# The float32 first chunk of a fused attention, Fourier-mixing and FFN kernel made one token tile instead of two, the leftover tile put last, and the sums of the weights' squares given a PSUM bank of their own

## The chip, the cores and the metric

The kernel runs on one NeuronCore of a Trainium2 chip, as one launch. The metric is the device time of the launch in microseconds (us). The engines of the core work side by side, each through a queue of its own in a fixed order: PE (TensorE: matmuls, with the weight loads PEld beside them), DVE (VectorE), ACT (ScalarE), POOL (GpSimd) and SP (SyncE, which only issues transfers here). An instruction starts when those ahead of it on its engine are through and the semaphores that it waits for have come.

## The reference, cut to what matters

```
a    = softmax(phi over the sequence)                 # B=8, H=8, S=576, M=32
k_m  = a^T k ;  v_m = a^T v                           # 32 memories a head
attn = softmax(q k_m^T / sqrt(64)) v_m                # -> x: (8, 576, 512)
u    = x + real(FFT over the sequence, then over the 512 features)
un   = (u - mean(u)) / sqrt(var(u) + 1e-6)            # over the features
out  = u + relu(un @ w_ch1) @ w_ch2                   # 512 -> 2048 -> 512
```

All inputs are float32 and so is the output. 8 x 576 tokens make 36 tiles of 128 tokens.

## The kernel before, in words

**Number formats.** Most products are made of float16 pairs: each operand is a high part and a low part, and three matmuls (high-high, high-low, low-high) stand for one. Both weights must for that be split into pairs, after a scaling by a power of two that is found from the sum of their squares. This takes time at the start, so the first chunk of the FFN, chunk 0, is computed in float32 straight from the unsplit weights.

**The weights.** `w_ch1` and `w_ch2` come in 8 slices each (j = 0 to 7, 128x1024 elements), as 64-bit words that are taken apart. `prepare_w1(j)` and `stage_w2(j)` call `to_f32`: ACT (L931, L935) and DVE (L937, L941, L942, L951) put a float32 slice together, ACT squares it (L957), a matmul with a matrix of ones adds the squares over the partitions (`all_sum`, L240), and `norm_scale` (L258, L266, L269 on DVE) makes the scale. `split_w1(j)` writes the float16 pair of a `w_ch1` slice (high on ACT L973, low on DVE L974), `prepare_w2` that of a `w_ch2` slice (high on ACT L1004, low on DVE L1009, or on POOL for the slices in `L2`). The scale of `w_ch2` (`scale_w2`, L993 to L997) needs all 16 sums. Three staging areas are reused from slice to slice, so that a load waits for the DVE to be through with an earlier slice.

**The FFN.** The 36 tiles are taken in chunks of `CH = 2`, 18 chunks. For each j, `ffn1` makes 256 hidden features (tile `ph`, pool `ps1` with two buffers), an eviction writes them as a float16 pair to `hring` (ACT L870, then DVE L871), and `ffn2` adds their part to the output (`po`, pool `ps2` with two buffers, one for each tile). In chunk 0 `ffn1_direct` and `ffn2_direct` do this in float32, with one ACT eviction (L830). `finish` adds `u` (DVE L892) and sends the tile out.

**The background.** `background` is a generator that makes the tiles `u`, batch by batch: pooling weights (`pf`, `pt_e`), memories (`pm`), scores (`psc`), value transforms (`pv`), spectra (`pa`, copied to `at` by ACT L686 and DVE L688; `vh` likewise from `pv` by L651 and L652), and the mixing (`pp`, `px`, added by DVE L755 and L769). `advance` moves it on between FFN steps. `norm_chunk` normalises a chunk's tiles (`norm_tile`) and transposes them. Batches 0 and 1 keep float32 in the memories and scores. The PSUM pool `psg` (4 buffers, tag `g`) is the ring of all of these; the sums of squares, `as_sq`, take a buffer of it each.

**Order.** A scheduler (with a model of its own of the engines) fixes the order of each engine's queue; `issue_after` and the lists `GATE1`, `GATE2`, `SUMS` and `EARLY` put instructions behind named marks, such as `un1`, the normalisation of tile 1. `keep_busy` issues matmuls whose result nobody uses, to fill TensorE early in the program.

Of the kernel before, what the change touches and what calls it, by code (L numbers as in the profile page):

```python
# [46 lines left out]
GATE1[2] = ["un1", "uh0"]  # L47
SUMS = {8: ["as1_6", "as2_6"], 9: ["as1_7", "as2_7"]}
GATE2 = [[], ["un1", "qs0"]] + [["un1", f"ev{j - 2}"] for j in range(2, 8)]
# [88 lines left out]
def kernel(  # L138
# [659 lines left out]
    def norm_chunk(c):  # L798

        unT = unring[:, c % 2]  # L800
        unT0 = unT.rearrange("p l t k c -> p (l t k c)").bitcast(F32)
        unT0 = unT0.rearrange("p (k t c) -> p k t c", k=NK, t=CH)
        for i in range(CH):
            idx = CH * c + i
            norm_tile(idx, us[idx], un[:, i])
            if c == 0:
                pt = psg.tile([P, 512], F32, tag="g", name=f"pt_unT_{i}")
                for k in range(NK):
                    nc.tensor.transpose(pt[:, k * P : (k + 1) * P], un[:, i, k * P : (k + 1) * P], identf)
                marks["uh0"] = nc.scalar.copy(out=unT0[:, :, i], in_=pt.rearrange("p (k c) -> p k c", k=NK))  # L810
        if c == 0:
            return unT0
        marks[f"uh{c}"] = nc.scalar.copy(out=ud[:, 0], in_=un)  # L813
        marks[f"ul{c}"] = (nc.vector if c == 1 else nc.gpsimd).tensor_tensor(out=ud[:, 1], in0=un, in1=ud[:, 0], op=ALU.subtract)  # L814
        transpose(
            unT.rearrange("p l t k c -> p (l t k) c"), ud.rearrange("p l t c -> p (l t c)"), False, f"unT_{c}"
        )
        return unT

    def ffn1_direct(j):  # L820

        w = w1_f32(j).rearrange("p (k c) -> p k c", k=NK)
        h = h_f32(j)
        for f in range(UB):
            ph = ps1.tile([P, CH, P], F32, tag="h", name=f"ph_0_{j}_{f}", padded_shape=[P, 4, P])
            for k in range(NK):
                marks[f"f1_{j}"] = nc.tensor.matmul(  # L827
                    ph, lhsT=w[:, k, f * P : (f + 1) * P], rhs=unTs[0][:, k], start=(k == 0), stop=(k == NK - 1)
                )
            marks[f"ev{j}"] = nc.scalar.activation(h[:, f], ph, AF.Relu)  # L830
# [4 lines left out]
    def h_f32(j):  # L835
        h = hring[:, 4 + j % 2].rearrange("p l f c -> p (l f c)").bitcast(F32)
        return h.rearrange("p (f t c) -> p f t c", f=UB, t=CH)

    def ffn2_direct(j, po):
        w = w2_f32(j).rearrange("p (a c) -> p a c", a=UB)  # L840
        h = h_f32(j)
        for f in range(UB):
            for t in range(CH):
                marks[f"f2_{j}"] = nc.tensor.matmul(  # L844
                    po[t],
                    lhsT=h[:, f, t],
                    rhs=w[:, f],
                    start=(j == 0 and f == 0),
                    stop=(j == NW - 1 and f == UB - 1),
                )  # L850

    def ffn1(c, unT, j, hs):

        ph = ps1.tile([P, UB, CH, P], F32, tag="h", name=f"ph_{c}_{j}")
        mm = groups()
        for f in range(UB):
            i = 0
            for k in range(NK):
                for lw, lu in ((0, 0), (0, 1), (1, 0)):
                    mm(  # L860
                        ph[:, f],
                        lhsT=w1t[:, j, lw, k, f * P : (f + 1) * P],
                        rhs=unT[:, lu, :, k],
                        start=(i == 0),
                        stop=(i == 3 * NK - 1),
                    )
                    i += 1
        h = h_slot(c, j)
        phv = ph.rearrange("p f t c -> p (f t) c")
        marks[f"ev{c}_{j}"] = nc.scalar.activation(h[:, 0], phv, AF.Relu)  # L870
        nc.vector.scalar_tensor_tensor(  # L871
            out=h[:, 1], in0=phv, scalar=0.0, in1=h[:, 0], op0=ALU.max, op1=ALU.subtract
        )
        hs.append(h)

    def ffn2(c, j, hs, po):
        for f in range(UB):
            for t in range(CH):
                for i, (lh, lw) in enumerate(((0, 0), (0, 1), (1, 0))):
                    nc.tensor.matmul(  # L880
                        po[t],
                        lhsT=hs[j][:, lh, f * 2 + t],
                        rhs=w2s[:, j * UB + f, lw, :],
                        start=(j == 0 and f == 0 and i == 0),
                        stop=(j == NW - 1 and f == UB - 1 and i == 2),
                    )

    def finish(c, po):
        for t in range(CH):
            idx = CH * c + t  # L890
            u = us.pop(idx)
            nc.vector.scalar_tensor_tensor(out=u, in0=po[t], scalar=cout if c else 0.5, in1=u, op0=ALU.mult, op1=ALU.add)  # L892
            nc.sync.dma_start(out=out[idx], in_=u)
# [30 lines left out]
    def to_f32(stages, dst, key):  # L924
# [51 lines left out]
    def prepare_w1(j):  # L976
# [4 lines left out]
        with tc.issue_after(marks["un1"].ins):  # L981
# [5 lines left out]
    def stage_w2(j):  # L987
        top = to_f32(parts_w2.pop(j), w2_f32(j), f"2_{j}")
        with tc.issue_after(marks["un1"].ins):
# [23 lines left out]

    marks = {}
    held = [False]
    ahls = {}
    us = {}
    n_tiles = B * S // P
    n_chunks = n_tiles // CH
# [3 lines left out]
    def background():  # L1023
# [3 lines left out]
        for b in range(B):  # L1027
# [24 lines left out]
            for step in range(NG + 2) if b > 0 else ():  # L1052
# [25 lines left out]
            for t in (0, 1, 2) if b % 2 == 0 else (2, 0, 1):  # L1078
                yield nt, 2 if t < 2 else 1 - b % 2
                if t == 2:  # L1080
                    if b % 2 == 0:
# [3 lines left out]
                        nt += 1  # L1085
# [4 lines left out]
                    add_mix(u2, rows, px, igx, tm, 0)  # L1090
                    continue
                pp = ahead or mix_pp(b, f"t{t}", slice(t * P, (t + 1) * P), full, at, vh)
                ahead = None
                tm = mix_m(full, *pp, isg, isg)
                for sign in range(2):
                    c0 = (2 * t + sign) * P
                    px = mix_x(b, f"t{t}{sign}", c0, P, full, attnT, vbd)
# [5 lines left out]
                if b == 0 and t == 0:  # L1103
                    with tc.issue_after(marks["px"].ins):
                        ahead = mix_pp(b, "t1", slice(P, 2 * P), full, at, vh)
                    keep_busy(28, 2 * P, "norm", behind=marks["pp"])
# [36 lines left out]
    gate = ["un1", "uh0"]  # L1143
# [8 lines left out]
    while made < 2:  # L1152
# [5 lines left out]
    po = [ps2.tile([P, 512], F32, tag="o", name=f"po_0_{t}") for t in range(CH)]  # L1158
    for j in range(NW):
# [9 lines left out]
        if made >= 2 * CH and 1 not in unTs:  # L1169
# [19 lines left out]
    advance(CH, CH * 3)  # L1189
    unTs[2] = norm_chunk(2)  # L1190
    for n in range(NW, n_steps):
        c, j = divmod(n, NW)
        if j == 0:
            po = [ps2.tile([P, 512], F32, tag="o", name=f"po_{c}_{t}") for t in range(CH)]
        ffn2(c, j, hs[c], po)
        run_ffn1(n + 4 if n + 4 <= 2 * NW else n + NHS)
        if j < NW - 1:
            advance(CH * c, steps=1)
        else:
            finish(c, po)  # L1200
            if c + 2 < n_chunks:
                advance(CH * (c + 1), CH * (c + 3))
# [65 lines left out]
```

## Time and profile before

| what | value |
| --- | --- |
| device time, median of 3 runs | 946.54 us (946.08 to 947.56) |
| the profiled execution's own time | 946.59 us |
| its span, first to last instruction | 944.7 us |
| mean granted TensorE clock | 0.996 |
| busy: PE / PEld / DVE / ACT / POOL | 931.0 / 660.5 / 575.8 / 465.2 / 222.7 us |
| first float32 matmul of chunk 0 (`ph` L827) | 55.47 us after the span's start |
| first float16 matmul of chunk 1 (`ph` L294) | 130.6 us |
| first low part of a `w_ch2` slice (DVE L1009) | 144.75 us |
| last matmul ends | 940.2 us |

The profiled execution is within 0.05 us of the median, and 1.9 us of its time lie around its span. Times of instructions are counted from the span's start. A line number stands for a line of the kernel before, unless the text says that it is of the changed kernel. L294 is the line of a helper that issues matmuls in groups, so the tile's name tells what is computed there. "PE busy" counts a matmul from start to a modelled end; matmuls overlap, so the time that one takes in a full queue is that of a stretch divided by its count.

### The profile page before, as it was taken

The numbers are of one execution on the slowest core, as the hardware profiler recorded it, in microseconds if no ns is written. First come the engines' busy times: TensorE is split into PE (matmuls) and PEld (weight loads), VectorE is DVE, ScalarE is ACT, GpSimd is POOL, SyncE is SP. The second block draws the span as 40 slices with busy tenths as digits, with TensorE's granted clock in tenths as the row PEclk, the third lists the DMA queues.
The fourth block names the chain that finished last, engine by engine and source line by source line (L and its number), as shares of the span: only waits on it lengthen the run. The fifth ranks groups of instructions, "written<-read, shape, count | busy, mean of one in ns | idle before, by whom it ended". The sixth has DMA issues, their size and how long they took to land.

```text
span 944.7 us, 18855 instructions
## 1 busy us (share of the span) xinstructions
PE 931.0 (99%) x7742; PEld 660.5 (70%) x7742; DVE 575.8 (61%) x1309; ACT 465.2 (49%) x917; POOL 222.7 (24%) x251
## 2 busy tenths in 40 slices
PE   7899999999999999999999999999999999999998
PEld 6666786777767677677667767776776777666664
DVE  4899997777677766676424766677646675211111
ACT  4577568765476537554414554655445544211110
POOL 2300142324133313333100422334122242100000
PEclk9899999999999999999999999999999999999999
DMA  9944650355246423645104541374215321100000
GB/s 345 377 199 124 232 146 17 81 146 115 51 94 136 115 49 59 169 95 95 23 24 97 136 102 37 70 160 115 49 24 128 64 51 35 46 17 28 1 23 23
DMA packets 131320, 92.02 MB, mean 97 GB/s; under 512 B 115745, under 2 KB 115745, under 8 KB 129185
## 3 DMA queue, kind: packets, MB, share of 16 engines
q1 hardware_dynamic: 131088, 90.77, 37.5%
q8 instruction: 61, 1.00, 0.4%
q14 instruction: 27, 0.21, 0.1%
q10 hardware_dynamic: 144, 0.03, 0.0%
HBM read 58.15 MB, written 9.44 MB: 72 GB/s over the span
## 4 chain that ended last, share of the span: by engine, by line
PE 96%; DVE 2%; ACT 1%; DMA 0%; POOL 0%; issue 0%; SPq 0%; DVEq 0%; ACTq 0%
PE ph L294 38%; PE po L880 37%; PE pm L294 4%; PE ph L827 3%; PE po L844 3%; PE psc L294 2%; PE pp_t L294 2%; PE pv L644 1%; PE px_t L294 1%; PE pa L674 1%; PE pp_t L738 1%; PE pf L375 1%; PE pa L666 0%; DMA phs<-in_raw 0%; PE busy_fold L252 0%
## 5 line engine op out<-in xcount | busy, mean ns | idle before, releaser
L294 PE MATMUL ph<-unring,w1t 128*128 128x256 f16 x3264 | 389.7, 273 | 0.0
L880 PE MATMUL po<-w2s,hring 128*128 128x512 f16 x1632 | 379.1, 379 | 0.0
L294 PEld LDWEIGHTS <-w1t 128*128 128x128 f16 x3324 | 318.8, 98 | 62.4 <-issue 1.2
L880 PEld LDWEIGHTS <-hring 128*128 128x128 f16 x1632 | 156.8, 98 | 157.4 <-issue 0.2
L871 DVE SCALAR_TENSOR_TENSOR hring<-ph,hring 128x512 f16<-128x512 f32 x136 | 93.2, 686 | 151.0 <-ACT hring L870 150.4
L870 ACT ACTIVATE hring<-ph 128x512 f16<-128x512 f32 x136 | 80.1, 590 | 156.7 <-PE ph L294 156.2
L574 POOL TENSOR_TENSOR aring<-aring,scratch 128x384 f32<-128x384 f32 x30 | 24.9, 832 | 249.5 <-DVE scratch L572 227.1
L793 POOL TENSOR_TENSOR scratch<-scratch,small 128x1 f32<-128x1 f32 x36 | 21.1, 588 | 157.4 <-DVE scratch L792 153.7
L294 PEld LDWEIGHTS <-stg 128*128 128x128 f16 x1152 | 44.8, 98 | 9.4 <-issue 0.8
L814 POOL TENSOR_TENSOR ud<-un,ud 128x1024 f16<-128x1024 f32 x16 | 34.0, 2127 | 38.9 <-ACT ud L813 38.9
L509 ACT CAST aeo<-eo 128x384 f16<-128x384 f32 x30 | 15.3, 511 | 53.8 <-DVE eo L506 53.8
L566 ACT ACTIVATE aring<-aring,scratch 128x384 f32<-128x384 f32 x24 | 14.6, 610 | 50.0 <-DVE aring L563 50.0
L502 DVE TENSOR_TENSOR eo<-aring 128x128 f32<-128x128 f32 x29 | 35.4, 1220 | 3.7 <-POOL aring L591 3.6
L294 PE MATMUL pm<-et,stg 128*128 128x64 f16 (+1 forms) x780 | 37.1, 199 | 0.0
L755 DVE SCALAR_TENSOR_TENSOR share<-pp_t,scratch,small 128x257 f32<-128x257 f32 (+1 forms) x48 | 21.1, 481 | 25.0 <-ACT small L751 25.0
L554 DVE TENSOR_REDUCE scratch<-psc 128x12 f32<-128x384 f32 x32 | 17.6, 551 | 30.1 <-PE pm L294 19.1
L591 POOL TENSOR_TENSOR aring<-aring 128x128 f32<-128x128 f32 x60 | 34.8, 600 | 2.3
L769 DVE SCALAR_TENSOR_TENSOR uring<-px_t,scratch,share 128x256 f32<-128x256 f32 (+1 forms) x80 | 34.0, 477 | 0.3 <-PE px_t L294 0.2
L586 POOL TENSOR_TENSOR hring<-aring,hring 128x640 f16<-128x640 f32 x24 | 34.2, 1424 | 0.1
L450 POOL TENSOR_TENSOR stg<-rawt,stg 128x640 f16<-128x640 f32 x12 | 17.2, 1432 | 72.0 <-ACT rawt L449 72.0
L813 ACT CAST ud<-un 128x1024 f16<-128x1024 f32 x17 | 17.8, 1046 | 28.4 <-DVE un L794 18.5
L827 PE MATMUL ph<-unring,w1t 128*128 128x256 f32 x128 | 30.6, 383 | 0.7 <-ACT unring L810 0.7
(262 smaller groups left out, 1284.3 us busy)
## 6 DMA issues: line engine op xcount, KB each, us to landing
rawt<-in_raw SPq DMA_DIRECT2D x15, 640.0 KB, 4.7
stg<-in_raw SPq DMA_DIRECT2D x15, 640.0 KB, 4.3
out<-uring SPq DMA_DIRECT2D x36, 256.0 KB, 2.1
stg<-in_w SPq DMA_DIRECT2D x7, 1024.0 KB, 6.2
rawt<-in_raw SPq DMA_DIRECT2D x15, 384.0 KB, 3.4
stg<-in_raw SPq DMA_DIRECT2D x15, 384.0 KB, 3.1
phs<-in_raw SPq DMA_DIRECT2D x32, 160.0 KB, 4.7
w2s<-in_w SPq DMA_DIRECT2D x4, 1024.0 KB, 10.4
```

What stands on the lines that cost most here:

```text
L294: m = nc.tensor.matmul(out, lhsT=lhsT, rhs=rhs, start=start, stop=stop)
L502: nc.vector.tensor_tensor(out=eo[:, 0, 1:3], in0=ap[:, 1:3, 0], in1=ap[:, 1:3, 1], op=ALU.add)
L574: eng.tensor_tensor(out=a, in0=a, in1=sm.unsqueeze(2).to_broadcast([P, 12, M]), op=ALU.mult)
L586: nc.gpsimd.tensor_tensor(out=ahw[:, :, :, 1], in0=a10, in1=ahw[:, :, :, 0], op=ALU.subtract)
L591: eng.tensor_tensor(out=a2[:, i : i + 4], in0=a[:, 0:4], in1=a[:, 4:8], op=op)
L769: nc.vector.scalar_tensor_tensor(out=u[rows, hs], in0=px[rows, hs], scalar=igx[rows], in1=tm[rows, w * NJ + half : w * NJ + half + 256], o ...
L814: marks[f"ul{c}"] = (nc.vector if c == 1 else nc.gpsimd).tensor_tensor(out=ud[:, 1], in0=un, in1=ud[:, 0], op=ALU.subtract)
L827: marks[f"f1_{j}"] = nc.tensor.matmul(ph, lhsT=w[:, k, f * P : (f + 1) * P], rhs=unTs[0][:, k], start=(k == 0), stop=(k == NK - 1))
L844: marks[f"f2_{j}"] = nc.tensor.matmul(po[t], lhsT=h[:, f, t], rhs=w[:, f], start=(j == 0 and f == 0), stop=(j == NW - 1 and f == UB - 1),)
L870: marks[f"ev{c}_{j}"] = nc.scalar.activation(h[:, 0], phv, AF.Relu)
L871: nc.vector.scalar_tensor_tensor(out=h[:, 1], in0=phv, scalar=0.0, in1=h[:, 0], op0=ALU.max, op1=ALU.subtract)
L880: nc.tensor.matmul(po[t], lhsT=hs[j][:, lh, f * 2 + t], rhs=w2s[:, j * UB + f, lw, :], start=(j == 0 and f == 0 and i == 0), stop=(j == NW ...
```

## The change

Chunk 0, the float32 one, is now tile 0 alone. Chunks 1 to 17 hold tiles 1 and 2, 3 and 4, and so on, and a new chunk 18 holds tile 35 alone, in float16 pairs like the others. `tiles(c)` gives a chunk's tiles, and the loops run over them. Where marks stood at `un1` they stand at `un0`; the background yields after tile 0, before the second half of the first mixing is added to tile 1; the hold on it at the end of batch 1's scores is gone. `ffn1_direct` takes both halves of a slice into one bank and evicts them together. The second buffer of `ps2`, which chunk 0 has no use for any more, is called `sums` and takes the 16 sums of squares, one column each.

```
-GATE1 = [[], ["un1", "qs0"]] + [["un1", f"ev{j - 2}"] for j in range(2, 8)]
-EARLY = {"1_0": ["kmf0_0", "sub0_0"], "2_0": ["at0", "un1"]}
+GATE1 = [[], ["un0", "qs0"]] + [["un0", f"ev{j - 2}"] for j in range(2, 8)]
+EARLY = {"1_0": ["kmf0_0", "sub0_0"], "2_0": ["at0", "un0"]}
...
+        ph = ps1.tile([P, UB, P], F32, tag="h", name=f"ph_0_{j}", padded_shape=[P, 4, P])
+        mm = groups()
         for f in range(UB):
-            ph = ps1.tile([P, CH, P], F32, tag="h", name=f"ph_0_{j}_{f}", padded_shape=[P, 4, P])
             for k in range(NK):
-                marks[f"f1_{j}"] = nc.tensor.matmul(
-                    ph, lhsT=w[:, k, f * P : (f + 1) * P], rhs=unTs[0][:, k], start=(k == 0), stop=(k == NK - 1)
+                marks[f"f1_{j}"] = mm(
+                    ph[:, f], lhsT=w[:, k, f * P : (f + 1) * P], rhs=unTs[0][:, k], start=(k == 0), stop=(k == NK - 1)
                 )
-            marks[f"ev{j}"] = nc.scalar.activation(h[:, f], ph, AF.Relu)
+        marks[f"ev{j}"] = nc.scalar.activation(h_f32(j), ph, AF.Relu)
...
-            for t in range(CH):
-                marks[f"f2_{j}"] = nc.tensor.matmul(
-                    po[t],
-                    lhsT=h[:, f, t],
-                    rhs=w[:, f],
-                    start=(j == 0 and f == 0),
-                    stop=(j == NW - 1 and f == UB - 1),
-                )
+            marks[f"f2_{j}"] = nc.tensor.matmul(
+                po[0], lhsT=h[:, f], rhs=w[:, f], start=(j == 0 and f == 0), stop=(j == NW - 1 and f == UB - 1)
+            )
...
-            top = all_sum(sq[:, 0:1], 1, f"sq_{key}")
+            top = all_sum(sq[:, 0:1], 1, f"sq_{key}", sums[0], 2 * j + int(key[0]) - 1)
...
+    def tiles(c):
+        return range(n_tiles)[max(CH * c - 1, 0) : CH * c + 1]
...
-    n_chunks = n_tiles // CH
+    n_chunks = n_tiles // CH + 1
...
-                    held[0] = (b, step) == (1, NG)
+                    held[0] = False
...
-    po = [ps2.tile([P, 512], F32, tag="o", name=f"po_0_{t}") for t in range(CH)]
+    po = [ps2.tile([P, 512], F32, tag="o", name="po_0_0")]
+    sums.append(ps2.tile([P, 512], F32, tag="o", name="sums"))
...
-        if made >= 2 * CH and 1 not in unTs:
+        if made > CH and 1 not in unTs:
             unTs[1] = norm_chunk(1)
```

The orders of the queues move with it. Two places matter for what follows. In the names, the number behind `ph_0_` or `ph_1_` is the slice j (before, the two halves of a slice follow it in chunk 0), `pm_1_` and `psc_1_` are the memories and scores of batch 1 by pair of heads, and the last number is only a counter.

PE, in the float32 stage, slice 5 of chunk 0. Before:

```order
L827 MATMUL ph_0_5_0_1115<-unring_101,w1t_97 128x256 x4
L827 MATMUL ph_0_5_1_1121<-unring_101,w1t_97 128x256 x4
L294 MATMUL pm_1_0_859<-et_71,rawt_68 128x64 x10
L844 MATMUL po_0_0_664<-w2s_98,hring_103 128x512
L844 MATMUL po_0_1_665<-w2s_98,hring_103 128x512
```

PE at the same place of the changed kernel:

```order
L357 MATMUL pt_e1_1_826<-identf_84,phs_69 128x128 x4
L359 MATMUL pl_1_1_794<-identf_84,phs_69 64x128
L294 MATMUL pm_1_0_869<-et_71,rawt_68 128x64 x10
L294 MATMUL ph_0_5_1060<-unring_101,w1t_97 128x128 x8
L240 LDWEIGHTS small_83
L240 MATMUL sums_652<-scratch_108,small_83 128x1
L294 MATMUL psc_1_0_884<-scratch_108,rawt_68 128x64 x6
L294 MATMUL pm_1_1_938<-et_71,stg_96 128x64 x10
L849 MATMUL po_0_0_651<-w2s_98,hring_103 128x512 x2
```

A slice of chunk 0 is now eight matmuls of 128 columns and two of 512, instead of eight of 256 and four of 512; batch 1's memories and scores and the sums of squares stand between the slices.

DVE, at the first low part of a `w_ch2` slice (L1009). Before, it stands directly behind the eviction of slice 3 of chunk 1, and the copies of the spectra and of `pv` (`at`, `vh`) follow it:

```order
L996 RECIPROCAL small_83<-small_83 128x1
L516 SCALAR_TENSOR_TENSOR aeo_74<-aeo_74,small_83,eo_80 128x2x64
L997 TENSOR_SCALAR small_83<-small_83 128x8
L871 SCALAR_TENSOR_TENSOR hring_103<-ph_1_3_1373,hring_103 128x512
L1009 SCALAR_TENSOR_TENSOR w2s_98<-w2s_98,small_83 128x2x512
L688 SCALAR_TENSOR_TENSOR at_77<-pa_1_0_0_1430,at_77 128x2x145
L688 SCALAR_TENSOR_TENSOR at_77<-pa_1_0_1_1440,at_77 128x2x145
L652 SCALAR_TENSOR_TENSOR vh_76<-pv_1_0_1412,vh_76 128x512
```

DVE at the same place of the changed kernel, where that line is L1010 and the eviction's is L873:

```order
L652 SCALAR_TENSOR_TENSOR vh_76<-pv_1_1_1184,vh_76 128x512
L516 SCALAR_TENSOR_TENSOR aeo_74<-aeo_74,small_83,eo_80 128x2x64
L688 SCALAR_TENSOR_TENSOR at_77<-pa_1_0_0_1193,at_77 128x2x145
L688 SCALAR_TENSOR_TENSOR at_77<-pa_1_0_1_1203,at_77 128x2x145
L996 TENSOR_SCALAR small_83<-small_83 128x1
L502 TENSOR_TENSOR eo_80<-aring_78 128x128
L503 SCALAR_TENSOR_TENSOR eo_80<-aring_78,small_83 128x64
L506 TENSOR_TENSOR eo_80<-aring_78 128x192
L997 RECIPROCAL small_83<-small_83 128x1
L873 SCALAR_TENSOR_TENSOR hring_103<-ph_1_3_1448,hring_103 128x512
L998 TENSOR_SCALAR small_83<-small_83 128x8
```

The next row of that queue is the first low part. Two copies of `vh` (the other stands just above) and two of `at` are now ahead of it, and the evictions of chunk 1's slices 0 to 3 are as before. Between the first addition of the mixing to tile 0 (DVE L769 on `px_0_t00`) and this place the two queues hold the same instructions by kind and size, but for these four, which are added, and one `finish` of chunk 0 (L892), which is gone: 205 instructions before, 208 now.

More of the change, by code (lines that the diff above doesn't have):

```diff
@@ L801, in norm_chunk @@
         unT0 = unT.rearrange("p l t k c -> p (l t k c)").bitcast(F32)
-        unT0 = unT0.rearrange("p (k t c) -> p k t c", k=NK, t=CH)
-        for i in range(CH):
-            idx = CH * c + i
+        unT0 = unT0[:, : NK * P].rearrange("p (k c) -> p k c", k=NK)
+        n = len(tiles(c))
+        for i, idx in enumerate(tiles(c)):
             norm_tile(idx, us[idx], un[:, i])
@@ L877, in ffn2 @@
         for f in range(UB):
-            for t in range(CH):
+            for t in range(len(po)):
                 for i, (lh, lw) in enumerate(((0, 0), (0, 1), (1, 0))):
@@ L888, in finish @@
     def finish(c, po):
-        for t in range(CH):
-            idx = CH * c + t
+        for t, idx in enumerate(tiles(c)):
             u = us.pop(idx)
@@ L980, in prepare_w1 @@
         s = s1[:, j : j + 1]
-        with tc.issue_after(marks["un1"].ins):
+        with tc.issue_after(marks["un0"].ins):
             norm_scale(s, is1[:, j : j + 1], top, 1, 9, f"w1_{j}")
@@ L988, in stage_w2 @@
         top = to_f32(parts_w2.pop(j), w2_f32(j), f"2_{j}")
-        with tc.issue_after(marks["un1"].ins):
+        with tc.issue_after(marks["un0"].ins):
             norm_scale(s2[:, j : j + 1], is2[:, j : j + 1], top, 1, 14, f"w2_{j}")
@@ L1011, in prepare_w2 @@
                 )
+    def tiles(c):
+        return range(n_tiles)[max(CH * c - 1, 0) : CH * c + 1]
     marks = {}
     held = [False]
+    sums = []
     ahls = {}
@@ L1078, in background @@
             for t in (0, 1, 2) if b % 2 == 0 else (2, 0, 1):
-                yield nt, 2 if t < 2 else 1 - b % 2
+                yield nt, (2 if b or t else 1) if t < 2 else 1 - b % 2
                 if t == 2:
@@ L1102, in background @@
                     nt += 1
[L1103 to L1106, printed above, removed]
+                    px = None
+                    if nt == 1:
+                        px = mix_x(b, f"t{t}1", P, P, full, attnT, vbd)
+                        with tc.issue_after(marks["px"].ins):
+                            ahead = mix_pp(b, "t1", slice(P, 2 * P), full, at, vh)
+                        keep_busy(28, 2 * P, "norm", behind=marks["pp"])
+                        yield nt, 1
             yield nt, 0
@@ L1141, in after @@
             return fn(*a)
-    gate = ["un1", "uh0"]
+    gate = ["un0", "uh0"]
     def advance(done, upto=n_tiles, steps=None):
@@ L1150, in advance @@
             steps = steps and steps - 1
-    while made < 2:
+    while made < 1:
         made, room = next(bg)
@@ L1188 @@
         run_ffn1(NW + 1 + j)
-    advance(CH, CH * 3)
+    advance(1, tiles(2).stop)
     unTs[2] = norm_chunk(2)
@@ L1193 @@
         if j == 0:
-            po = [ps2.tile([P, 512], F32, tag="o", name=f"po_{c}_{t}") for t in range(CH)]
+            po = [ps2.tile([P, 512], F32, tag="o", name=f"po_{c}_{t}") for t in range(len(tiles(c)))]
         ffn2(c, j, hs[c], po)
@@ L1197 @@
         if j < NW - 1:
-            advance(CH * c, steps=1)
+            advance(tiles(c).start, steps=1)
         else:
@@ L1201 @@
             if c + 2 < n_chunks:
-                advance(CH * (c + 1), CH * (c + 3))
+                advance(tiles(c + 1).start, tiles(c + 2).stop)
                 unTs[c + 2] = norm_chunk(c + 2)
```

40 lines of the change are left out of this document (23 added, 17 removed).

## The prediction

> **What bounds the kernel now.** I read the page first: the busy times and the chain that ended last.
>
> ```profile
> span 944.7 us, 18855 instructions
> PE 931.0 (99%) x7742; PEld 660.5 (70%) x7742; DVE 575.8 (61%) x1309; ACT 465.2 (49%) x917; POOL 222.7 (24%) x251
> PE 96%; DVE 2%; ACT 1%; DMA 0%; POOL 0%; issue 0%; SPq 0%; DVEq 0%; ACTq 0%
> ```
>
> As an average over the span, the kernel is TensorE's. But the change takes its work out of one stage, so the table by stage comes next (columns: PE, PEld, DVE, ACT and POOL busy us, granted clock, DMA share, GB/s).
>
> ```profile
> 49.07:144.75 95.68, 93.62 (x559) 69.95 (x557) 89.36 (x207) 66.04 (x114) 16.70 (x25) 1.00 0.54 171
> 144.75:940.00 795.25, 795.21 (x6816) 556.31 (x6813) 453.62 (x1021) 374.12 (x758) 191.06 (x195) 1.00 0.33 72
> ```
>
> From 144.75 us on TensorE never rests and DVE has 43% to spare. In the first stage, from the mixing's first addition to tile 0 to the first low part of `w_ch2`, two engines are full: PE 93.62 of 95.68 us, DVE 89.36. DVE stands idle there for 6.3 us in all. The two ends are these rows of the timeline:
>
> ```profile
> 49.07 1.65 DVE L769 SCALAR_TENSOR_TENSOR uring<-px_t,scratch,share 128x256 f32<-128x256 f32 x4
> 144.75 1.29 DVE L1009 SCALAR_TENSOR_TENSOR w2s<-w2s,small 128x1024 f16<-128x1024 f32 x1 [0.62 <-ACT w2s L1004]
> ```
>
> What DVE still waits for, from the table of waits between 44 and 150 us (us in total, times, longest):
>
> ```profile
> DVE eo L503 <- POOL aring L574: 1.0, 1, 1.0
> DVE scratch L258 <- PE as_sq L240: 0.9, 3, 0.4
> DVE w2s L941 <- ACT w2s L931: 0.7, 1, 0.7
> DVE scratch L570 <- ACT aring L566: 0.6, 1, 0.6
> DVE un L794 <- POOL scratch L793: 0.5, 1, 0.5
> DVE scratch L422 <- PE pm L294: 0.3, 1, 0.3
> ```
>
> Only 1.2 us of these are waits for TensorE (0.9 and 0.3).
>
> **What the change takes from TensorE and gives back.** The chain in order of time (start, us, what) has the prices:
>
> ```profile
> 83.43 3.48 PE po L844 x8
> 86.90 3.45 PE ph L827 x16
> 65.65 0.92 PE px_t L294 x16
> 98.34 2.18 PE pm L294 x20
> 133.38 2.64 PE ph L294 x24
> 930.47 9.73 PE po L880 x45
> ```
>
> A float32 slice of two tiles costs 3.45 us (`ph`) and 3.48 us (`po`). With one tile `po` halves to 1.74. For `ph` the question is whether its weight loads let the matmul of 128 columns go at half the time; the nearest row is `pm`, float32 with 64 columns: 2.18 / 20 = 109 ns a pass. `ph` at 256 columns takes 3.45 / 16 = 216 ns a pass, half of which is 108, so the loads just keep up: 1.73 us. Saved: 8 x (1.73 + 1.74) = 27.7 us. Bounds: nothing of `ph` saved gives 13.9, all gives 27.7.
>
> Chunk 18 comes on top, in float16 pairs: 192 matmuls of 128 columns and 48 of 512. Half of 2.64 / 24 is 55 ns, the `px` row with its own 128 columns gives 0.92 / 16 = 57.5 ns, so 10.6 to 11.0 us; `po` takes 9.73 / 45 = 216 ns, so 10.4. Together 21.2 us, all of it at the end, where TensorE has nothing else to do. TensorE's own account is 6.5 us shorter.
>
> **What DVE does meanwhile.** That account only counts if TensorE has work for the 27.7 us that come free. In the float32 stage each slice waits for DVE to put the weights together; then chunk 1's evictions hold TensorE back, since `ph` has two buffers: `ph` of slice k starts when the eviction of slice k - 2 is through on DVE. And `po` of chunk 1 needs the first low part of `w_ch2` (L1010). In the changed queue DVE has the same work ahead of that place, but for two copies of `at` and two of `vh` more and one `finish` less. Their rows, by groups between 44 and 150 us (count, busy us, mean ns):
>
> ```profile
> L652 DVE SCALAR_TENSOR_TENSOR vh<-pv,vh 128x512 f16<-128x512 f32 x4 | 2.7, 684 | 2.7 <-ACT vh L651 2.7
> L688 DVE SCALAR_TENSOR_TENSOR at<-pa,at 128x290 f16<-128x290 f32 x4 | 1.7, 486 | 0.0
> L892 DVE SCALAR_TENSOR_TENSOR uring<-po,uring 128x512 f32<-128x512 f32 x2 | 1.4, 686 | 0.0
> ```
>
> By busy time that is 2 x 0.43 + 2 x 0.68 - 0.7 = +1.5 us. So L1010 cannot start before 49.07 + 89.36 + 1.5 = 139.9 us, with every idle moment of DVE closed, and with none closed it starts at 146.3. I take 144.0: the 1.2 us of waits for TensorE go, and about 1 us of the others is covered by better mixing of batch 1's scores with the weights; the rest are relays between ACT, POOL and DVE, whose steps the change leaves as they are. Hence 0.75 us earlier than before.
>
> How far is TensorE by then? Its changed queue has chunk 1's slices 0 to 5 ahead of the first `po` of chunk 1. Slice 5 needs slice 3's eviction, which on DVE ends about 0.5 us ahead of L1010 (one L516 and one small row between); slice 5 takes 2.6, so TensorE is there 2.1 us after L1010. Before, at 144.75, it had done this:
>
> ```profile
> 143.51 0.98 PE ph L294 x8
> 144.49 0.76 PE pv L644 x5
> 940.22 0.75 DVE uring L892
> ```
>
> that is, slices 0 to 3 and a third of slice 4, and was in the middle of `pv`. The changed one is ahead by 40 matmuls of 110 ns and some `pv`: 4.7 us. From there on both have the same work, without gaps before, plus chunk 18. The last `finish` has one addition instead of two: 0.7 us less, by the last row.
>
> The sum for the end: -0.75 (L1010 earlier) + 2.1 - 4.7 + 21.2 - 0.7 = +17.2 us. The profiled execution took 946.59 us, 0.05 more than the median, so 963.7, rounded to 963.5. Seen from TensorE: of the 27.7 us nearly all become idle time, and 21.2 are paid at the end.
>
> Edits costed at nothing. The float32 start moves some 1.5 to 2 us forward, since tile 0 no longer waits for tile 1's addition and norm; it then waits for the weights, so DVE's queue covers it. The sums' own bank frees buffers of the ring, but no row above shows a wait for one; `po_1` takes that bank only after the last sum is read, ten microseconds earlier on DVE. ACT evicts half as many elements in chunk 0; it is busy for 66.04 of 95.68 us, no bound. SP issues the same loads in the same order: each staging area comes free by DVE. If the cover in the end stage fails (two buffers of `ph`, evictions now of 256 elements), TensorE waits there; a slice's 2.7 us against under 1.5 us of ACT and DVE speaks against it.
>
> **The rivals.**
>
> *Carried through (faster).* TensorE's account decides: -6.5 - 0.7 gives 939.4. The average speaks for it: PE 99%. The Trainium skill, "Perfetto Trace Analysis", section "Identifying the Most-Contended Engine", would have the engine of highest occupancy treated first, which here is PE over the span; its section "Optimization Strategy" adds that a kernel may have several regimes. Against it speaks the stage's row: DVE would have to reach L1010 at about 126.8 us for no change at all (144.0 - 17.2), 13 us less than its own busy time allows. It can win only if TensorE had more to do ahead of that point than I found. Chance 0.06.
>
> *Gain in part.* DVE closes nearly all of its gaps and TensorE finds something more: 949 to 957. Chance 0.09. No change within 0.2% (1.9 us, about what a measurement of this kernel can tell from none) lies between this and the first: 0.02.
>
> *New waits, and the clock.* TensorE now rests for some 24 us in the stage. The profile shows what a long rest does:
>
> ```profile
> 34.00:38.00 4.00, 1.11 (x12) 0.66 (x10) 3.83 (x14) 2.77 (x7) 1.51 (x3) 0.89 1.01 401
> 40.00:44.00 4.00, 4.00 (x22) 2.10 (x21) 1.43 (x3) 1.54 (x3) 0.52 (x1) 0.51 0.94 266
> 8.00:10.00 2.00, 1.08 (x11) 0.79 (x8) 1.65 (x9) 1.15 (x5) 0.00 (x0) 1.00 1.01 401
> ```
>
> After 2.9 idle us of 4 the clock was 0.51 for some six microseconds; with 0.92 idle of 2 it stayed at 1.00. Between two slices TensorE may now rest 3 to 4 us (a slice every 7 to 8 us on DVE, 3.5 us of its own work), near that edge. At half clock 6 us of work cost 12; where the stage has slack this hides, but DVE's sums wait behind it: two such falls that reach DVE's queue cost 6 us, 969.5, and waits of DVE behind its in-order queue may add as much: 967 to 975. Chance 0.15. The Trainium skill, "TensorE: Matmul & The Clock Gate", section "Part 1: The HAM clock gate", says that an idle window of about 3.4 us halves the clock and as much sustained work restores it; the 0.51 above agrees with the half, and by that rule the gaps here would fall on either side.
>
> *As forecast:* 957 to 967. Chance 0.68. That the change does not do what it says is excluded by the queue: `ph_0` has 128 columns.
>
> **How the numbers follow.** Likeliest: 963.5 us. Its own range is 139.9 to 146.3 for L1010, 959.6 to 966.0, with 2 us for the rest. The range for 8 in 10 takes in part of the rival with new waits and of the gain in part: 954.5 to 971. Faster 0.06, same 0.02, slower 0.92.
>
> **What would show it.** Right: TensorE busy for 65 to 70 us of the 90 us ahead of L1010, with waits on DVE in the slices; L1010 at 140 to 146 us; DVE over 93% busy there; no gap from 150 us on; 21 us for chunk 18. The float32 `ph` slice at 1.7 us shows the halving. Wrong: L1010 below 135 us, or TensorE waiting past 150 us, or a clock of 0.5 in the float32 stage.

## The result, and the profile after

| kernel | median of 4 runs | ratio to before | span / mean clock of its profiled execution |
| --- | --- | --- | --- |
| before | 946.81 us (946.08 to 947.56) | | 944.7 us / 0.996 |
| changed | 958.62 us (958.01 to 965.89) | 1.0142 [1.0093, 1.0192] | 964.0 us / 0.984 |
| changed, run a second time | 959.59 us (959.35 to 961.49) | 1.0139 [1.0124, 1.0155] | 957.8 us / 0.990 |

The change costs 12 to 13 us. Forecast were 963.5 us, 17 more than before. The profiled execution of the first row of the changed kernel is by chance the longest of its four, 965.89 us; the second set, of the same code, left a profile at its median. That one, called the second profile below, is read first, and the long execution is set against it at the end. Line numbers are those of the changed kernel from here on.

The page of the second profile, its span, its busy times and the chain that ended last:

```profile
span 957.8 us, 19281 instructions
PE 931.5 (97%) x7946; PEld 665.5 (69%) x7946; DVE 569.9 (60%) x1317; ACT 466.6 (49%) x917; POOL 229.7 (24%) x252
PE 87%; DVE 7%; ACT 3%; issue 1%; POOL 1%; DVEq 0%; ACTq 0%; POOLq 0%
```

TensorE is busy for as long as before (931.5 against 931.0 us), and the span is 13.1 us longer: it rests for 26.3 us, where it rested for 13.7. DVE's share of the chain goes from 2 to 7%. Where the rest lies is seen in the table by stretches (length, then PE, PEld, DVE, ACT and POOL busy us, granted clock, DMA share, GB/s). The second profile:

```profile
60.00:80.00 20.00, 11.54 (x59) 8.52 (x58) 20.00 (x52) 11.53 (x21) 4.14 (x3) 0.89 0.66 256
80.00:100.00 20.00, 17.15 (x104) 14.09 (x103) 18.34 (x44) 17.07 (x33) 0.00 (x0) 0.85 0.74 198
100.00:120.00 20.00, 20.00 (x148) 16.68 (x148) 20.00 (x47) 13.46 (x22) 4.88 (x6) 1.00 0.73 225
120.00:140.00 20.00, 17.47 (x147) 13.70 (x146) 18.91 (x53) 11.70 (x20) 11.72 (x16) 0.91 0.41 119
48.05:139.42 91.37, 76.97 (x550) 61.69 (x548) 87.85 (x210) 65.06 (x108) 21.30 (x25) 0.93 0.57 177
139.42:935.00 795.58, 795.01 (x6856) 557.31 (x6854) 446.31 (x1020) 374.96 (x758) 193.43 (x196) 1.00 0.32 73
```

and the kernel before in the first of these stretches:

```profile
60.00:80.00 20.00, 20.00 (x109) 14.14 (x108) 19.25 (x39) 14.09 (x23) 1.52 (x2) 1.00 0.65 263
```

Two thirds of the new rest, 8.5 us, lie at 60 to 80 us, where DVE is busy without a break; 2.9 follow at 80 to 100 and 2.5 at 120 to 140. From 139.42 us to the last chunk TensorE is full again (795.01 of 795.58), as it was before. So the float32 work that was taken out came free in a stage where DVE had hardly any to give up: it is busy for 87.85 of 91.37 us there, 96%.

The end of that stage and the float32 slice, from the timeline of the second profile (start, us, engine, line, operation, count, and the idle time before it):

```profile
139.38 1.28 DVE L1010 SCALAR_TENSOR_TENSOR w2s<-w2s,small 128x1024 f16<-128x1024 f32 x1 [0.96 <-ACT w2s L1005]
141.03 0.59 PE L882 MATMUL po<-w2s,hring 128*128 128x512 f16 x2
102.39 2.03 PE L294 MATMUL ph<-unring,w1t 128*128 128x128 f32 x16
104.26 1.45 PE L294 MATMUL psc<-scratch,stg 128*128 128x64 f32 x12
113.25 1.94 PE L849 MATMUL po<-w2s,hring 128*128 128x512 f32 x4
115.02 0.17 PE L240 MATMUL sums<-scratch,small 128*128 128x1 bf16 x1
```

The first low part of `w_ch2` starts 5.4 us earlier than before (139.38 against 144.75), and `po` of chunk 1 follows 1.65 us behind it. From start to start a float32 `ph` slice of one tile takes 1.87 us and its `po` 1.77: the halving of `ph` holds within 0.14 us. Chunk 18 runs at one slice in 2.64 us:

```profile
939.26 1.50 PE L294 MATMUL ph<-unring,w1t 128*128 128x128 f16 x24
940.61 1.46 PE L882 MATMUL po<-w2s,hring 128*128 128x512 f16 x6
941.90 1.50 PE L294 MATMUL ph<-unring,w1t 128*128 128x128 f16 x24
```

What the forecast's sum did not have is in the table of waits, PE from 48 to 200 us of the second profile (us in total, times, longest):

```profile
PE sums L240 <- DVE scratch L258: 6.8, 4, 3.3
PE ph L294 <- DVE w1t L952: 2.5, 3, 1.0
PE po L849 <- DVE scratch L784: 1.6, 1, 1.6
PE pt_e L357 <- ACT phs L354: 1.0, 2, 0.5
```

The first row is a wait that the change brought: a sum of squares is not written into the bank `sums` before DVE's L258 has read the sum ahead of it from the same bank. The first three rows, all waits for DVE, make 10.9 of the 14.4 us that TensorE rests between 48.05 and 139.42 us. One of the four places of the first row, 2.53 us long, holds up the first float16 slices:

```profile
123.48 0.18 PE L240 MATMUL sums<-scratch,small 128*128 128x1 bf16 x1 [2.53 <-DVE scratch L258]
```

### The profile page after: what moved, and what is told of

It reads as the page before. It is cut to its first block, busy times and chain, and to the rows that moved or that the text cites. A ratio compares the mean times of both kernels' runs of the same rounds, so it can differ in the third digit from the quotient of the medians.

```text
span 964.0 us, 19281 instructions
## 1 busy us (share of the span) xinstructions
PE 938.1 (97%) x7946; PEld 670.6 (70%) x7946; DVE 570.3 (59%) x1317; ACT 466.7 (48%) x917; POOL 229.8 (24%) x252
## 4 chain that ended last, share of the span: by engine, by line
PE 89%; DVE 5%; ACT 3%; issue 1%; POOL 1%; DMA 0%; SPq 0%; DVEq 0%; ACTq 0%
PE ph L294 38%; PE po L882 37%; PE pm L294 4%; PE psc L294 2%; PE pp_t L294 2%; PE pa L674 1%; PE pv L644 1%; PE px_t L294 1%; PE pp_t L738 1%; PE po L849 1%; PE pf L375 0%; PE pa L666 0%; DVE uring L769 0%; DVE w2s L952 0%; DMA phs<-in_raw 0%
## 5 line engine op out<-in xcount | busy, mean ns | idle before, releaser
L294 PE MATMUL ph<-unring,w1t 128*128 128x256 f16 (+2 forms) x3584 | 424.5, 272 | 2.8 <-DVE w1t L952 2.5
L882 PE MATMUL po<-w2s,hring 128*128 128x512 f16 x1680 | 391.3, 379 | 0.6 <-ACT hring L872 0.6
L294 PEld LDWEIGHTS <-w1t 128*128 128x128 f16 (+1 forms) x3516 | 331.1, 98 | 66.1 <-issue 1.3
L882 PEld LDWEIGHTS <-hring 128*128 128x128 f16 x1680 | 160.8, 98 | 161.0 <-ACT hring L872 1.1
L873 DVE SCALAR_TENSOR_TENSOR hring<-ph,hring 128x512 f16<-128x512 f32 (+1 forms) x144 | 96.7, 672 | 170.0 <-ACT hring L872 169.3
L872 ACT ACTIVATE hring<-ph 128x512 f16<-128x512 f32 (+1 forms) x144 | 83.3, 578 | 184.4 <-PE ph L294 183.9
L793 POOL TENSOR_TENSOR scratch<-scratch,small 128x1 f32<-128x1 f32 x36 | 23.8, 660 | 154.8 <-DVE scratch L792 139.3
L814 POOL TENSOR_TENSOR ud<-un,ud 128x1024 f16<-128x1024 f32 (+1 forms) x17 | 35.2, 2071 | 46.2 <-ACT ud L813 46.2
L769 DVE SCALAR_TENSOR_TENSOR uring<-px_t,scratch,share 128x256 f32<-128x256 f32 (+1 forms) x80 | 34.0, 476 | 0.1
L755 DVE SCALAR_TENSOR_TENSOR share<-pp_t,scratch,small 128x257 f32<-128x257 f32 (+1 forms) x48 | 21.1, 480 | 21.7 <-ACT small L751 21.5
L893 DVE SCALAR_TENSOR_TENSOR uring<-po,small,uring 128x512 f32<-128x512 f32 x35 | 25.0, 742 | 10.7 <-PE po L882 10.7
L516 DVE SCALAR_TENSOR_TENSOR aeo<-aeo,small,eo 128x128 f16<-128x128 f16 x30 | 24.5, 816 | 11.0 <-ACT aeo L509 11.0
```

Source lines behind the costliest of these rows:

```text
L294: m = nc.tensor.matmul(out, lhsT=lhsT, rhs=rhs, start=start, stop=stop)
L516: marks[f"s{b}_{g}"] = nc.vector.scalar_tensor_tensor(out=av4[:, 1, :, 0, gs], in0=av4[:, 0, :, 0, gs], scalar=mk[:, 64:65], in1=eo[:, :, ...
L769: nc.vector.scalar_tensor_tensor(out=u[rows, hs], in0=px[rows, hs], scalar=igx[rows], in1=tm[rows, w * NJ + half : w * NJ + half + 256], o ...
L873: nc.vector.scalar_tensor_tensor(out=h[:, 1], in0=phv, scalar=0.0, in1=h[:, 0], op0=ALU.max, op1=ALU.subtract)
L882: nc.tensor.matmul(po[t], lhsT=hs[j][:, lh, f * len(po) + t], rhs=w2s[:, j * UB + f, lw, :], start=(j == 0 and f == 0 and i == 0), stop=(j ...
```

## The experiments

Two theories are set against each other. **DVE paces the stage**: what is taken from TensorE ahead of 139 us becomes rest, and chunk 18 is paid in full. **New waits and the clock**: TensorE's rests are made by the waits that the change brought and by the falls of the clock behind them, and would go with these. Each ratio is to runs of the kernel before on the same chip: a median of 946.86 us (7 runs) for the changed kernel again, the one without chunk 18, the sums in the ring, and less work for DVE on the changed kernel; 947.52 (12) for half of the sums, less work on the kernel before, DVE's work to ACT, and the filled gaps; 946.97 (19) for the two kernels with still less work.

The scheduler works out the order of the queues anew for each edited kernel. Up to the first `po` of chunk 1 only the kernel without chunk 18 has the order of the changed kernel. That `po` stands behind six slices of chunk 1's `ph` in the changed kernel, behind four with the sums in the ring and in both changed kernels with less work for DVE, and behind three with half of the sums in the ring; DVE's order differs as well. So each of these runs shows an edit together with its order, and none holds the order fixed.

**The changed kernel again** (no edit).

> The changed kernel unaltered, for a second profile. The profiled execution of it took 965.89 us and three others 958.0 to 959.2; its clock fell to 0.50 to 0.87 between 70 and 110 us. Theory (VectorE paces the stage before the first low part of w_ch2; a fall of the clock comes on top where a rest of TensorE is long enough): 958 to 959 us where the clock falls less, with the first low part at 138 to 140 us instead of 145.6, and the same idle time of TensorE, 10 us or more before it. Rival (the spread lies in the stage after it, or in transfers): the first low part again at 145 us and the time lost later.

959.59 us, 1.0139 [1.0124, 1.0155]. The result stands, and its profile is the one above: the first low part at 139.38 us, where the theory put it, and 14.4 us of rest ahead of it.

**Only chunk 18 left out.** Tile 35 goes out without its FFN.

```
-    n_chunks = n_tiles // CH + 1
+    n_chunks = n_tiles // CH
...
+    nc.sync.dma_start(out=out[n_tiles - 1], in_=us[n_tiles - 1])
```

> The changed kernel without chunk 18: tile 35 is sent out as it comes from the mixing, with no FFN. It prices the chunk of one tile at the end. Theory (it lies wholly on the path, 192 matmuls of 55 to 57 ns and 48 of 216 ns): 20 to 22 us less than the changed kernel, 936 to 939 us. Rival (some of it is hidden behind the last full chunk): 10 to 15 us less.

937.78 us, 0.9907 [0.9892, 0.9922]: 21.8 us less than the changed kernel. The term of 21.2 us is right to 0.6, and nothing of the chunk is hidden. Without it the change saves 9 us of the 27.7 (`ph` and `po` in float32) that TensorE's account gives it.

**The sums of squares back in the ring.**

```
-            top = all_sum(sq[:, 0:1], 1, f"sq_{key}", sums[0], 2 * j + int(key[0]) - 1)
+            top = all_sum(sq[:, 0:1], 1, f"sq_{key}")
...
-    sums.append(ps2.tile([P, 512], F32, tag="o", name="sums"))
```

> The changed kernel, but the sums of squares back in the ring of the attention's buffers, so that the second bank of ps2 lies idle. Theory (VectorE's queue sets the pace, no row shows a wait for a ring buffer): the same within 2 us, 957 to 961 us. Rival (the bank of their own is what keeps the stage from being worse): 965 us or more.

969.74 us, 1.0246 [1.0229, 1.0263], 10 us slower than with the bank; the theory of 957 to 961 us failed. The forecast gave the bank nothing. The two places in this kernel's timeline:

```profile
142.08 1.28 DVE L1010 SCALAR_TENSOR_TENSOR w2s<-w2s,small 128x1024 f16<-128x1024 f32 x1
149.34 0.38 PE L882 MATMUL po<-w2s,hring 128*128 128x512 f16 x1
```

L1010 is 2.7 us later than with the bank, and `po` of chunk 1 comes 7.3 us behind it instead of 1.65. TensorE does not wait for L1010 here: it works off mixing and `ph` slices that stand ahead of `po`. At that `po` it has 812.5 us to go to its last matmul, with the bank 812.8, so the loss is complete there. Its stretches say what kind of loss it is:

```profile
100.00:120.00 20.00, 16.53 (x122) 14.16 (x121) 17.52 (x49) 13.39 (x21) 5.38 (x6) 0.98 0.77 242
120.00:140.00 20.00, 16.83 (x110) 12.96 (x110) 17.35 (x57) 11.28 (x24) 11.02 (x16) 0.68 0.49 127
```

Here neither engine is full: DVE loses 2.5 us at 100 to 120 that it works through with the bank, TensorE 3.5. In this kernel the sums stand on PE in pairs (two `as_sq` matmuls together at 95.27, 104.26 and 113.21 us). The longest of TensorE's waits from 48 to 200 us is for weights that DVE puts together:

```profile
PE ph L294 <- DVE w1t L952: 5.2, 2, 4.8
```

No row of that table can be put down to a buffer of the ring with certainty. Whether the order of the queues or the held buffers cost the 10 us was not taken apart.

**Half of the sums in the ring.** Those of `w_ch1` keep the bank, those of `w_ch2` take the ring, which halves the users of the wait at L258.

```
-            top = all_sum(sq[:, 0:1], 1, f"sq_{key}", sums[0], 2 * j + int(key[0]) - 1)
+            top = all_sum(sq[:, 0:1], 1, f"sq_{key}", *([sums[0], j] if key[0] == "1" else []))
```

> The changed kernel with the sums of w_ch1 in the bank of their own and those of w_ch2 back in the ring of the attention's buffers. In the changed kernel each sum waits until VectorE has read the one before it in the same bank; TensorE rests 6.8 us for that. Theory A (this wait costs): 1 to 3 us less than the changed kernel. Theory B (what counts is that sums hold buffers of the ring, which cost 10 us with all 16 in it): 3 to 7 us more, 962 to 966 us.

967.87 us, 1.0217 [1.0195, 1.0239], above even theory B's range. The wait for L258 is gone from TensorE's table of waits, and the kernel is 8 us slower, so removing that wait in this way does not help. What the wait costs by itself is not shown, since the edit puts eight sums in the ring and orders the queues anew. Eight sums in the ring cost nearly what sixteen do.

**Less work for DVE.** In ten slices of the weights DVE no longer puts the lowest bits in (one instruction of 1.2 us a slice, in two slices two halves of 0.7); the weights lose some precision by that. The same edit is made on both kernels.

```
-                nc.vector.scalar_tensor_tensor(
-                    out=part.bitcast(U32),
-                    in0=lo.bitcast(U32),
-                    scalar=29,
-                    in1=part.bitcast(U32),
-                    op0=ALU.logical_shift_right,
-                    op1=ALU.bitwise_or,
-                )
```

> The changed kernel without the VectorE instruction that puts the lowest three bits into ten of the sixteen weight slices (L943, 1.14 us from start to start, 11.4 us in all); these bits are left out of the weights. Theory (VectorE paces the stage): 7 to 11 us less, 947 to 951 us. Rival (TensorE's clock, ACT or the loads pace it): 0 to 3 us less.

> The kernel before, without the VectorE instruction that puts the lowest three bits into ten of the sixteen weight slices (11.4 us of VectorE; the bits are left out). On the changed kernel this gave 6.8 us. Theory (before, TensorE is full in that stage, so VectorE does not pace it): 0 to 1.5 us less than the kernel before, 945.3 to 946.8 us. Rival (VectorE paced both): 4 to 8 us less.

On the changed kernel 952.81 us, 1.0065 [1.005, 1.008]: 6.8 us less. On the kernel before 946.91 us, 0.9997 [0.9985, 1.0009]: nothing. DVE's work is worth something only since the change. But less came than was expected of the first (7 to 11 us): L1010 (here L1002) starts 12.1 us earlier than in the second profile and the kernel gains half of it. TensorE has done less by then: at the first `po` of chunk 1, 11.4 us earlier, it has 818.7 us to go to its last matmul instead of 812.8. The reason is in its stretches:

```profile
127.29 1.27 DVE L1002 SCALAR_TENSOR_TENSOR w2s<-w2s,small 128x1024 f16<-128x1024 f32 x1
60.00:80.00 20.00, 13.01 (x85) 9.73 (x83) 19.99 (x55) 15.03 (x26) 3.62 (x3) 1.00 0.75 266
80.00:100.00 20.00, 19.75 (x119) 14.68 (x118) 18.62 (x45) 20.00 (x37) 0.00 (x0) 0.91 0.81 228
```

TensorE's rest at 60 to 80 us shrinks only from 8.5 to 7.0 us, since DVE is still full there: the work that went lies mostly behind it. And at 80 to 100 ACT is now full as well.

**Still less.** Beside the above, the instruction that sets the sign (L952) goes in all 16 slices, so that the weights lack their signs; again on both kernels.

```
-            with early(key, 1):
-                marks[key] = nc.vector.scalar_tensor_tensor(
-                    out=d, in0=hi, scalar=-0x80000000, in1=d, op0=ALU.bitwise_and, op1=ALU.bitwise_or
-                )
```

> The changed kernel with VectorE taken far out of the way: without the instruction for the lowest three bits in ten slices (11.4 us, left out in lessdve too) and without the one for the signs in all sixteen (18 us more); weights without signs and low bits are multiplied. Of VectorE's 91 us ahead of the first low part of w_ch2 some 29 go. Theory (the change pays as soon as TensorE need not rest for VectorE; its own work is 6.5 us less): 940 to 945 us, below the kernel before. Rival (ACT, full from 80 to 100 us in lessdve, or the loads pace the stage next): 948 to 952 us, hardly less than lessdve's 952.8.

> The kernel before with the same left out (low bits in ten slices, signs in all sixteen). Theory (TensorE is full in that stage, whatever VectorE does): 945 to 947 us, as the kernel before. Rival (VectorE holds it back after all): 940 us or less.

The changed kernel takes 944.75 us, 0.9982 [0.9971, 0.9992] of the kernel before; the kernel before with the same edit 946.45 us, 0.9994 [0.9984, 1.0003]. So 29 us of DVE's work (569.9 to 540.8 by the page) bring the one 14.8 us and the other nothing. It is the test that decides most: with DVE relieved the change stops costing time, and the sign of its effect turns. The new order of the queues, which both relieved kernels have too, was not held apart. The first stretches of the relieved kernel, and one of the relieved kernel before:

```profile
60.00:80.00 20.00, 17.20 (x93) 11.80 (x92) 14.88 (x57) 19.94 (x37) 1.09 (x2) 0.91 0.77 250
80.00:100.00 20.00, 20.00 (x148) 17.00 (x147) 13.83 (x33) 18.45 (x32) 3.38 (x4) 1.00 0.84 278
```

```profile
80.00:100.00 20.00, 20.00 (x92) 14.29 (x90) 5.53 (x14) 11.76 (x27) 0.00 (x0) 1.00 0.67 218
```

In the changed kernel TensorE's rest at 60 to 80 is down from 8.5 to 2.8 us and none is left at 80 to 100; ACT is full now. In the kernel before DVE stands idle for 14.5 of 20 us and TensorE is no faster for it.

**DVE's work moved to ACT.** ACT makes the upper bits in all 16 slices instead of 6, which takes one DVE instruction away in each of ten.

```
-LA = ["1_0", "2_0", "1_1", "2_1", "1_2", "2_2"]
+LA = [f"{i}_{j}" for j in range(8) for i in (1, 2)]
```

> The changed kernel with the other way of putting a slice together for all 16 slices instead of 6 (ACT takes the upper bits, L936, 1.2 us more of ACT for each; VectorE has one instruction less, L942, 0.6 us from start to start): VectorE 6 to 7 us less over ten slices, ACT 11 to 12 us more. Theory (VectorE paces): 3 to 5 us less, 954 to 956 us. Rival (ACT, then busy for over 80% of the stage, paces instead): the same or more.

962.89 us, 1.0157 [1.0132, 1.0183]: no gain, where the theory had 3 to 5 us. The interval overlaps that of the changed kernel, so a loss is not shown either. In one stretch ACT is now the engine that is full:

```profile
80.00:100.00 20.00, 13.50 (x68) 8.28 (x67) 17.43 (x40) 20.00 (x33) 0.38 (x1) 0.91 0.59 184
```

With ACT at 20.00 of 20 DVE is down to 17.43, and TensorE to 13.50. That ACT then paces the stage is read from this row, not tested.

**TensorE kept busy in the gaps.** 16 matmuls whose result nobody uses ahead of each of slices 2 to 6, in the half of the `ph` bank that a single tile leaves free.

```
+        if 2 <= j <= 6:
+            keep_busy(16, 2 * P, f"f{j}", pb[:, UB:].rearrange("p f c -> p (f c)"))
```

> The changed kernel with 16 matmuls of 256 columns, whose result nobody uses, ahead of each of slices 2 to 6 of chunk 0, in the idle half of the slice's bank: 80 in all, 8.7 us at full clock, where TensorE rested for some 11 us. Theory (the rests let the clock fall, which costs 5 us: mean clock 0.990 against 0.996): clock 0.995 or more and 2 to 5 us less, 954.5 to 957.5 us. Rival (the slow clock is hidden behind VectorE, and the fillers stand in the way): the same or up to 4 us more.

958.71 us, 1.0123 [1.0101, 1.0144]. The mean clock rises from 0.990 to 0.996, that of the kernel before, and the time falls by 0.9 us between the medians, with intervals that overlap: a gain that cannot be told from none, where the theory had 2 to 5 us. In the account below, 4.5 us of rest became 3.9 us of work. In the stage the clock stood at 0.50 for 13.65 us in the second profile and for 3.41 us here. Had the lost work been on the path, it would have been worth some 5 us, by half of the 10.2 us between them. So it was mostly hidden under waits for DVE, or the fillers took as much; the runs do not tell these apart.

**The account of all profiles**, from their pages. Rest is the span less PE busy; at a low clock the same work counts as more busy time.

| kernel | span | PE busy | rest | mean clock |
| --- | --- | --- | --- | --- |
| before | 944.7 | 931.0 | 13.7 | 0.996 |
| changed, second profile | 957.8 | 931.5 | 26.3 | 0.990 |
| changed, the long execution | 964.0 | 938.1 | 25.9 | 0.984 |
| chunk 18 left out | 936.4 | 909.8 | 26.6 | 0.989 |
| sums in the ring | 965.8 | 934.6 | 31.2 | 0.986 |
| half of the sums in the ring | 967.5 | 932.5 | 35.0 | 0.988 |
| DVE's work to ACT | 963.3 | 934.2 | 29.1 | 0.988 |
| gaps filled | 957.2 | 935.4 | 21.8 | 0.996 |
| less work for DVE | 952.4 | 928.5 | 23.9 | 0.992 |
| still less | 942.2 | 925.3 | 16.9 | 0.996 |
| kernel before, less work for DVE | 945.1 | 930.9 | 14.2 | 0.996 |
| kernel before, still less | 945.2 | 930.7 | 14.5 | 0.996 |

Chunk 18 moves busy time alone (21.7 us), the ring rest more than busy time. When DVE is relieved the changed kernel's rest goes from 26.3 to 16.9 us and its clock comes back; the kernel before keeps its rest.

## Why the prediction was right, point by point

**The mechanism** is as forecast: DVE bounds the stage, the freed float32 time becomes rest there, and chunk 18 is paid at the end. The runs with less work for DVE show it, by the pair of the changed kernel and the kernel before under the same edit, but for the order of the queues, which differs with the edit. The first of them alone, with half of what its DVE time would give, did not show it.

**The term that was mis-sized** is how much earlier L1010 starts: 0.75 us were taken ("I take 144.0"), between ends of 4.85 earlier (139.9) and 1.55 later. Measured were 5.4, past the lower end. The idle time of DVE, which was the disputed part, was near: 3.5 us are left in the stage, where 4.1 were taken. Two other things were not in the step. DVE is 1.0 us earlier already when the stage begins (48.05 against 49.07). That is not shown to come from the change: without chunk 18, with the same queues up to there, the stage begins at 49.98 us. And busy time does not add up: DVE's instructions overlap by a little, as three rows of the second profile show,

```profile
101.81 0.69 DVE L943 SCALAR_TENSOR_TENSOR w1t<-hring,w1t 128x512 uint32<-128x512 uint32 x1
102.41 0.69 DVE L943 SCALAR_TENSOR_TENSOR w1t<-uring,w1t 128x512 uint32<-128x512 uint32 x1
103.01 0.69 DVE L942 TENSOR_SCALAR w2s<-w2s 128x1024 int32<-128x1024 int32 x1
```

each 0.60 us behind the other and 0.69 long. Summed over the instructions of the stage, the durations grow by 1.5 us (103.0 to 104.5), which is what the forecast added for the change. But the busy time falls from 89.4 to 87.8, because the overlaps grow from 13.6 to 16.7: of 210 instructions 201 start before the one ahead has ended, where it was 167 of 207. So -1.0 (start) + 1.5 - 3.1 (overlap) - 2.8 (idle) = -5.4. That "L1010 cannot start before 139.9" was thus no bound. The rest of the sum held: with 5.4 and with `po` 1.65 us behind (2.1 taken), it gives -5.4 + 1.65 - 4.7 + 21.2 - 0.7 = +12.05, and the span of the second profile is 13.1 longer. Most of the last 1 us is the term of 0.7 for the second addition of the last `finish`, which did not come. The end of the kernel before, and that of the second profile:

```profile
930.30 10.52 PE L880 MATMUL po<-w2s,hring 128*128 128x512 f16 x48
940.22 1.41 DVE L892 SCALAR_TENSOR_TENSOR uring<-po,small,uring 128x512 f32<-128x512 f32 x2 [8.39 <-PE po L880]
948.51 5.34 PE L882 MATMUL po<-w2s,hring 128*128 128x512 f16 x24
953.89 0.75 DVE L893 SCALAR_TENSOR_TENSOR uring<-po,small,uring 128x512 f32<-128x512 f32 x1 [4.34 <-PE po L882]
```

Before, the first of the two additions lies beside the last matmuls, so one addition follows them in both kernels, and 3.9 us pass from the last matmul's end to the end of the span in both.

**The bank was costed at nothing, and that was wrong.** With the order of the queues that goes with it, it is worth 10 us. Without it L1010 starts 2.7 us earlier than before and `po` 7.3 us behind it, and the same sum gives -2.7 + 7.3 - 4.7 + 21.2 - 0.7 = +20.4; that kernel's span is 21.1 longer. The argument, that no row showed a wait for a buffer of the ring, was read from the kernel before, in which TensorE was full in that stage but for 2.1 us; it does not carry over to one in which it rests for 14.4. So 963.5 lies between the change without its bank and the one with it. That the long execution, at 965.89 us, comes near it is luck: its extra time is from the clock, as the last section shows.

**A wait that was missed.** The sums in one bank wait for DVE's read of the one before, 6.8 us in four places. The Trainium skill, "PSUM — Partial Sum Buffer", section "PSUM bank collisions raise a hardware error", says that a matmul must not write a bank while another engine reads it, even at other columns; by that the 16 columns of `sums` are one resource, and the row of waits agrees. The row shows the wait, not who asks for it. What it costs is not shown; 4.3 of the 6.8 us lie at 60 to 80 us, where DVE is full anyway.

**Where TensorE rests** was placed wrongly. It was to wait at the end of the stage, for slice 3's eviction on DVE. It does not: from 123.5 us on it is full up to the first `po` of chunk 1, and it rests mostly at 60 to 91 us, while DVE puts slices together and works on tile 1. The total of rest in the stage was 14.4 us against the 24 of the rival's text. Another 6.8 us, half of 13.65 us at a clock of 0.50, are work that counts as busy for twice its time (76.97 us busy against 65 to 70 expected).

**The signs that the forecast named.** Of those for being right, DVE over 93% busy (96%), no gap of note from 150 us on (0.57 us of waits in all) and 21 us for chunk 18 (21.8) came; L1010 at 140 to 146 us (139.38) and TensorE busy for 65 to 70 us (76.97) were missed by the second profile, and the float32 `ph` slice took 1.87 us instead of 1.7. One of those for being wrong came too: a clock of 0.50 in the float32 stage. It belongs to the rival with new waits and falls of the clock, so that rival is not refuted; it is a part of what happened.

**The rivals.** Carried through is refuted: it needed L1010 at 126.8 us. It came to 127.29 with less work for DVE, and even then the kernel was slower than before, because most of the rest at 60 to 80 us was still there, and TensorE had 5.8 us more to go at the first `po`; that point was thus not enough by itself. The gain in part, 949 to 957, was missed by 2 us. Its first half came, since DVE is through with the stage earlier; its second half, more work for TensorE, did not. New waits and falls of the clock are both there. Filling the gaps took most of the falls away and 0.9 us at most, which cannot be told from none; the waits were not priced alone. In one execution of eight a fall cost 6 us, which is the first point of the last section. ACT, "no bound" in the forecast, is full in one stretch of 20 us in each of the two changed kernels with less work for DVE.

## What to carry to other kernels

Before taking work from the engine that is full over the span, look at the stage that it leaves: if a second engine is nearly full there, as DVE was at 93%, the work that goes can turn to rest, while what is moved to the end was paid whole here. In such a stage the second engine's busy time before is not its lower bound: here a fuller queue ran its instructions closer together. And where 16 small sums are kept, with the order of the queues that followed from it, was worth 10 us, though the profile before showed no wait for these buffers; "no wait in the profile before" is not a price of zero.

## What the runs showed of the hardware

**The same code had falls of the clock of different length.** The long execution and the second profile have the same code and the same rests ahead of 92 us, and in both the clock falls to 0.50 shortly after, at 92.8 us. Their stretches of 2 us, the second profile first:

```profile
94.00:96.00 2.00, 2.00 (x11) 2.00 (x11) 1.54 (x5) 1.07 (x2) 0.00 (x0) 0.50 0.99 279
96.00:98.00 2.00, 2.00 (x19) 1.99 (x19) 0.81 (x2) 0.84 (x2) 0.00 (x0) 0.95 0.91 347
```

```profile
94.00:96.00 2.00, 2.00 (x10) 2.00 (x11) 1.73 (x8) 1.15 (x2) 0.00 (x0) 0.50 0.91 250
106.00:108.00 2.00, 2.00 (x4) 0.66 (x3) 2.00 (x4) 0.00 (x0) 0.00 (x0) 0.50 0.83 251
108.00:110.00 2.00, 2.00 (x9) 1.60 (x8) 1.87 (x5) 0.00 (x0) 0.00 (x0) 0.52 0.25 97
```

By the clock's record in the traces the fall lasts 3.41 us in the one and 17.07 in the other, five times as long, with TensorE busy in every one of the 2 us stretches from 94 us on. In all twelve profiles each fall that ends before the last matmul lasts one, two, three or five times 3.41 us. Nor does a fall need a long rest: in the 3.41 us ahead of the one at 92.80 us of the second profile TensorE was busy for 2.25. The float32 slices of the long execution show the half clock:

```profile
94.42 3.73 PE L294 MATMUL ph<-unring,w1t 128*128 128x128 f32 x16
104.88 3.73 PE L849 MATMUL po<-w2s,hring 128*128 128x512 f32 x4
```

The rows behind them start at 97.94 and 108.40 us, so from start to start each takes 3.52 us, where it was 1.87 and 1.77. The 13.7 us more at half clock are 6.8 us of work, by half of them, and the span is 6.2 longer. The delay reaches DVE's queue, and it is all there at the first low part, which starts 6.25 us later than in the second profile:

```profile
145.63 1.28 DVE L1010 SCALAR_TENSOR_TENSOR w2s<-w2s,small 128x1024 f16<-128x1024 f32 x1 [0.96 <-ACT w2s L1005]
```

The Trainium skill, "TensorE: Matmul & The Clock Gate", section "Part 1: The HAM clock gate", would have it back after about 3.4 us of sustained work: the second profile (3.41 us) agrees, the long execution (17.07) does not, and the measurement decides. Why is open; the work in these 17 us was nearly all float32, but so it was in the other execution.

**A float32 pass of 128 columns** takes 1.87 / 16 = 117 ns. With 256 columns it was 216 and with 64 it was 109: halving the columns takes 46% off the time once, and the second time 7%.

**Busy time of DVE depends on how full its queue is**, by the overlaps above: 66 ns an instruction before, 79 ns after. An instruction of a full queue thus starts a little before the one ahead is through. A sum of busy times from a trace with waits was no lower bound for the fuller queue here.
